# DeltaNet into soft MoE on one core: another order of VectorE's routing work and of the inverse's shares

## The chip, the cores and the metric

The kernel runs on one core of a Trainium2 chip. The metric is the device time of one execution in microseconds. A core has five engines that run side by side, each through its own queue in a fixed order: TensorE (PE, matrix products, with its weight loads as PEld), VectorE (DVE), ScalarE (ACT), GpSimd (POOL), and SyncE (SP), which here issues the DMA loads. An instruction that must wait for another engine holds up all that stands behind it in its own queue.

## The reference, cut to what matters

Two layers follow each other. The first is DeltaNet, a linear attention with a state that is corrected at every token, for 4 batches of 8 heads, 768 tokens and a head size of 48:

```python
k_n = k / (np.linalg.norm(k, axis=-1, keepdims=True) + 1e-06)
for t in range(S):
    y[:, :, t] = np.einsum('bhd,bhde->bhe', q[:, :, t], state)
    v_old = np.einsum('bhde,bhd->bhe', state, kt)
    state = state + bt[..., None] * np.einsum('bhd,bhe->bhde', kt, vt - v_old)
```

Its output, 3072 tokens of 384 numbers, is x of a soft mixture of experts with 8 experts of 4 slots:

```python
logits = x @ phi                                  # 3072 x 32
d = softmax(logits, axis=0)                       # over tokens, for each slot
slot_input = d.T @ x                              # 32 x 384
slot_out[e] = relu(slot_input[e] @ w1[e]) @ w2[e] # 384 -> 1024 -> 384
c = softmax(logits, axis=1)                       # over slots, for each token
out = c @ slot_out
```

(The two softmax lines are written short here; the reference subtracts the maximum, takes exp and divides by the sum plus 1e-9.)

## The kernel before

**Chunks and groups.** The 768 tokens are cut into 24 chunks of 32. The recurrence inside a chunk is written as a triangular system, so that a chunk needs one inverse for each of the 32 pairs of batch and head. Four chunks make a group (six groups, NG = 6), and one group's 4 x 32 inverses, of 32 x 32 each, are made at once on 128 partitions. Between chunks a state S is carried.

**A slot.** The main loop runs over x = 0 to 23. Slot x computes chunk x; c = x mod 4 is its place in the group. `chunk` (its functions stand in the listing) gives the steps of a chunk's own chain:

- `rest`: TensorE multiplies keys by the state (L481, into psR), then R = V - that product is formed. Where `turned_sign` holds, TensorE first adds -V into psR (L494) and ScalarE copies R (L498); elsewhere VectorE subtracts (L500). In groups 1 to 4 VectorE makes R at c = 0 and 1, ScalarE at c = 2 and 3; in group 0 it is the other way round; in group 5 VectorE always makes it.
- `read`: queries by the state (L481, into psY).
- `solve`: the inverse by R (L507, into psR), which ScalarE copies as U (L510).
- `update`: keys by U (L520, into psS), which ScalarE copies as the new state S (L527, two instructions). The next slot's `rest` needs it.
- `outputs`: the chunk's inner product (L537), copied by ScalarE as Y (L540).

Around this chain a slot prepares chunk x + 8 (transposes L261, products of keys and queries L290, their copies by ScalarE), scales the values of chunk x + 2 on GpSimd (`scale_v`, L442), masks the weights of chunk x + 1 on GpSimd (`weights`, L450), and copies the inverse of the next chunk on ScalarE (`solvers`, L458, from TT to Tbs).

**The inverse of a group on VectorE.** `invert(n)` makes some 90 small products and subtractions (lines 368 and 373: functions ea, es, ma, ms, then la, ls) in a fixed order. Before them come `spread` (a transpose of 128 x 1024 into lb, L325), `root` on ScalarE and `norms` (L343 to L355); two transposes into TT (`back`, L433) end it. `clear` sets the tile nm to zero on GpSimd once VectorE has last read it.

The inverse of group n + 2 is prepared at the last slot of group n (`spread`, `clear`, `root`) and its steps run in the four slots of group n + 1. The table `share` says what part of its estimated work stands at each of three places of each of the four slots; `plan` deals the steps out by it. The first place stands at the head of a slot, ahead of `rest`; the second after `solve`; the third later, with the hook "vec" in its middle. `norms` stands at the first slot's second place. What the shares leave over stands at the last slot's second place.

**Routing.** When a group's Y is complete, `route` works on its logits over the next six slots, as a list of six dictionaries: the entry's number is the slot after the group, its key the hook in the slot at which the functions are called. The hooks' order in a slot is head, (`rest`, `read`), sums, (`solve`), act, mid, vec, (`update`, `outputs`), end. On VectorE are `maxima` (L591, L592), `run_max` (L618, L622), `over_slots` (L628, L629), `shares` (L638 to L641) and `collect` (L703 to L707). ScalarE makes `rows_exp` and `slots_exp` (L648, L653, L634) of what run_max and over_slots give; shares sum and divide what slots_exp gives. `over_rows` (L597) and `slots` (L688) are products on TensorE.

The program's order is the order in which these calls are made: a manual schedule, with no planner that moves instructions. The loop calls them so:

```python
drain(EL[c][0]); hook("head")
rest(); read(); hook("sums"); solve()
...
hook("act"); drain(EL[c][1])
...
hook("mid"); drain(EL[c][2][:cut]); hook("vec"); drain(EL[c][2][cut:])
...
update(); outputs(); later(x, 2); hook("end")
```

After the loop come the two layers of the experts (L1038, L1061) and the output (L1119), whose weights are loaded into buffers as the loop sets them free.

Of the kernel before, what the change touches and what calls it, by code (L numbers as in the profile page):

```python
# [17 lines left out]
def kernel(  # L18
# [54 lines left out]
    def pt(shape):  # L73
        return ps.tile(shape, F32, name="pt", tag="pt", bufs=2)
# [490 lines left out]
    def route(n, Yn, yT, cs=range(GC), turn=None, behind=False):  # L565
# [114 lines left out]
        def slots(cs):  # L680

            pa = st["pa"] = [psS[:, cs[0] + y, 0:GD + 1] if n == NG - 1 else pt([P, GD + 1])
                             for y in range(2)]
            for c in cs:
                for b in range(B):
                    for y in range(2):
                        r, o = slice(64 * y, 64 * y + 64), slice(64 * (b % 2), 64 * (b % 2) + 64)
                        nc.tensor.matmul(  # L688
                            pa[y][o], lhsT=st["dr"][r, c * B + b].rearrange("p x s -> p (x s)"),
                            rhs=Yn[r, c, b, 0:GD + 1], start=(c == cs[0] and b < 2),  # L690
                            stop=(c == cs[-1] and b >= 2), skip_group_check=True)

            if not straight:
                st["pac"] = small.tile([P, 2, GD + 1], F32, name="pac", tag="pac", bufs=1)
                for y in range(2):
                    nc.scalar.activation(st["pac"][:, y], pa[y], ACT.Copy)

        def collect(first):
            parts = [(sacc[:, y], st["pa"][y]) for y in range(2)] if straight else [
                (sacc, st["pac"])]  # L700
            for s, pa in parts:
                if not first:
                    nc.vector.tensor_tensor(s, s, pa, op=ALU.add)  # L703
                elif turn == 0:
                    nc.vector.tensor_copy(s, pa)
                else:
                    nc.vector.scalar_tensor_tensor(s, s, st["al"], pa, op0=ALU.mult, op1=ALU.add)  # L707


        if n < NG - 2:  # L710
            return [dict(end=[logits]),
                    dict(head=[maxima], mid=[by_tokens], end=[over_rows]),
                    dict(head=[run_max, over_slots], end=[rows_exp, slots_exp]),
                    dict(act=[shares], end=[repeat, heads]),
                    dict(sums=[lambda: slots((0, 1))], vec=[lambda: collect(True)]),
                    dict(sums=[lambda: slots((2, 3))], vec=[lambda: collect(False)])]
        if n == NG - 2:
            return [dict(end=[logits]),
                    dict(act=[maxima], mid=[over_rows, by_tokens], vec=[run_max, over_slots],
                         end=[rows_exp, slots_exp]),  # L720
                    dict(act=[repeat, heads], vec=[shares],
                         mid=[lambda: slots((0, 1)), lambda: collect(True)],
                         end=[lambda: slots((2, 3)), lambda: collect(False)])]
# [14 lines left out]


    PLACES = 3  # L740
    share = [(0.0, 0.07, 0.16), (0.11, 0.10, 0.11), (0.09, 0.09, 0.09), (0.09, 0.09, 0.0)]

    def plan(n):

# [127 lines left out]
    def ends(x, name):  # L872

        if (x, name) == (NCH - 2, "end"):
            two[0] = route(NG - 1, Ys[1], yT[NG - 1], (0, 1), NG - 1)
            two[0]["logits"]()
        elif x == NCH - 1:
            for f in dict(head=["maxima"], act=["over_rows", "run_max", "rows_exp"],
                          mid=["repeat"], end=["heads"]).get(name, ()):
                two[0][f]()  # L880

    for x in range(NCH):
        n, c = divmod(x, GC)
        if c == 0 and n:
            routing[n - 1] = route(n - 1, Ys[(n - 1) % 2], yT[n - 1])
# [67 lines left out]
        if c == GC - 1:  # L953
            EL = empty
            if follow:
                f, EL = follow
                f["clear"]()
                f["root"]()

    rb = route(NG - 1, Ys[1], yT[NG - 1], (2, 3), NG, behind=True)  # L960
    Cn = [Call[:, i].rearrange("p b s -> p (b s)") for i in range(NG)]
    cT = cpool.tile([P, NG * P], F32, name="cT")
# [215 lines left out]
```

## Time and profile before

| what | value |
|---|---|
| time, median of 3 | 337.31 us (336.77 to 347.18) |
| the profiled execution | 342.02 us, span 340.3 us |
| TensorE busy | 280.8 us (83%) |
| VectorE busy | 212.2 us (62%) |
| ScalarE busy | 172.1 us (51%) |
| GpSimd busy | 155.9 us (46%) |
| mean granted TensorE clock | 0.876 |

A row of the timeline gives the start in us, the time that the instruction (or the merged run of equal ones, with its count) took, engine, line, operation, tiles and shapes; in brackets is how long the engine had sat idle before it, and what ended that. A row of the list of waits gives the waiting engine, line and tile, the engine and line waited for, and then the total in us, how often, and the longest in us. "PEclk" is the share of full clock that TensorE was granted, by fortieths of the span on the page (in tenths) and by stretch in the table of windows. PEld is the load of a matmul's stationary operand, which overlaps the matmuls; a wait can stand under PE and under PEld at once.

### The profile page before, as it was taken

What the parts mean: (1) busy time and instruction counts of PE and PEld (TensorE: products, weight loads), DVE (VectorE), ACT (ScalarE), POOL (GpSimd) and SP (SyncE); (2) the same over time, 40 slices, a digit from 0 to 9 for tenths busy, and PEclk for the clock granted to TensorE, in tenths of its full rate; (3) what the DMA queues carried; (4) which work ended last, traced back from release to release, by engine and by line L of the source; (5) the groups of instructions that cost most, each with busy time, mean ns of one, the idle gap of its engine ahead of it and who ended that gap; (6) DMA issues with size and microseconds to landing.
All of it is one profiled execution on the core that took longest, in us unless ns stands there. A gap on an engine that the chain in (4) does not pass through costs nothing.

```text
span 340.3 us, 16627 instructions
## 1 busy us (share of the span) xinstructions
PE 280.8 (83%) x7081; PEld 226.3 (66%) x7081; DVE 212.2 (62%) x807; ACT 172.1 (51%) x386; POOL 155.9 (46%) x336
## 2 busy tenths in 40 slices
PE   3996688888969889599886998939997888999981
PEld 3774476776858778477775877828876766636651
DVE  8599939875994478936769475697751221314341
ACT  3354254667724778156782646915475673221141
POOL 8966376559276078750599113994672000000000
PEclk9998559999965999759998589995799998999996
DMA  7866555454443246514520255526499559975196
GB/s 142 153 99 94 82 86 90 76 82 69 70 78 58 48 67 127 122 32 114 86 65 19 44 143 156 158 87 173 108 320 327 157 181 320 329 216 187 32 307 221
DMA packets 96378, 45.28 MB, mean 133 GB/s; under 512 B 75440, under 2 KB 89808, under 8 KB 96304
## 3 DMA queue, kind: packets, MB, share of 16 engines
q1 hardware_dynamic: 94512, 42.98, 50.9%
q0 software_dynamic: 704, 1.03, 1.6%
q8 instruction: 56, 0.92, 1.1%
q10 hardware_dynamic: 1088, 0.20, 0.3%
q14 instruction: 18, 0.15, 0.2%
HBM read 39.47 MB, written 4.72 MB: 130 GB/s over the span
## 4 chain that ended last, share of the span: by engine, by line
PE 53%; ACT 19%; DVE 16%; issue 4%; DMA 4%; POOL 1%; SPq 0%; DVEq 0%; POOLq 0%; ACTq 0%
PE psR L507 9%; PE psS L520 6%; PE pt L290 5%; DVE prs L368 5%; ACT S L527 5%; PE pt L261 4%; PE psY L537 4%; PE pt L558 4%; PE pso L1061 3%; PE ph L1038 3%; DVE prs L373 3%; PE psR L481 3%; ACT Tbs L458 2%; ACT dr L678 2%; PE psR L494 2%
## 5 line engine op out<-in xcount | busy, mean ns | idle before, releaser
L442 POOL TENSOR_SCALAR Vs<-Vs,nT 128x48 f32<-128x48 f32 x192 | 86.6, 475 | 24.0 <-DMA Vs<-in_v_dram 14.0
L450 POOL TENSOR_SCALAR_AFFINE_SELECT Abs<-GQ 32x256 f32<-32x256 f32 x96 | 48.2, 502 | 29.1 <-PE psY L537 24.4
L373 DVE TENSOR_TENSOR prs<-prs 128x16 f32<-128x16 f32 (+15 forms) x186 | 55.2, 297 | 0.4
L507 PE MATMUL psR<-R,Tbs 64*64 64x48 f32 x768 | 32.0, 241 | 20.5 <-DVE R L500 14.8
L368 DVE TENSOR_TENSOR prs<-tt,lb 128x96 f32<-128x96 f32 (+21 forms) x186 | 47.0, 290 | 0.0
L507 PEld LDWEIGHTS psR<-R,Tbs 64*64 64x64 f32 x768 | 28.9, 155 | 24.8 <-DVE R L500 16.4
L527 ACT ACTIVATE S<-psS 48x768 f32<-48x768 f32 x46 | 36.9, 803 | 8.7 <-PE psS L520 8.3
L510 ACT ACTIVATE U<-psR 128x384 f32<-128x384 f32 x24 | 11.8, 491 | 48.7 <-PE psR L507 42.4
L290 PE MATMUL pt<-KQ 48*32 48x64 f32 (+1 forms) x1792 | 27.2, 243 | 4.7 <-ACT KQ L277 3.2
L537 PE MATMUL psY<-U,Abs 64*64 64x48 f32 x768 | 30.5, 234 | 0.0
L537 PEld LDWEIGHTS psY<-U,Abs 64*64 64x64 f32 x768 | 27.4, 149 | 2.6 <-issue 0.8
L290 PEld LDWEIGHTS pt<-KQ 48*32 48x32 f32 x1792 | 21.8, 122 | 9.7 <-ACT KQ L277 5.0
L368 DVE TENSOR_TENSOR prs<-tt,prs 128x240 f32<-128x240 f32 (+14 forms) x90 | 26.0, 294 | 0.0
L320 POOL MEMSET prs<- 128x256 f32 x6 | 1.9, 314 | 51.4 <-DVE prs L368 51.4
L481 PEld LDWEIGHTS psR<-S,KQ 128*32 128x32 f32 x768 | 18.1, 120 | 10.8 <-ACT S L527 4.1
L373 DVE TENSOR_TENSOR tt<-tt,prs 128x30 f32<-128x30 f32 (+7 forms) x90 | 24.6, 273 | 0.0
L458 ACT ACTIVATE Tbs<-TT,own 128x256 f32<-128x256 f32 x48 | 21.6, 501 | 5.8 <-DVE TT L433 5.8
L481 PE MATMUL psY<-S,KQ 128*32 128x96 f32 x768 | 22.5, 256 | 2.0 <-issue 2.0
L481 PE MATMUL psR<-S,KQ 128*32 128x96 f32 x768 | 23.1, 267 | 1.0 <-ACT S L527 0.8
L294 ACT ACTIVATE GQ<-pt 128x256 f32<-128x256 f32 (+1 forms) x56 | 16.8, 351 | 13.2 <-PE pt L290 13.1
L558 PE MATMUL pt<-ident,Y 128*96 128x128 f32 x96 | 17.3, 306 | 6.8 <-ACT GQ L294 5.9
L261 PE MATMUL pt<-ident,Q 128*128 128x128 f32 x72 | 20.3, 315 | 0.0
(230 smaller groups left out, 602.5 us busy)
## 6 DMA issues: line engine op xcount, KB each, us to landing
Q<-in_q_dram SPq DMA_DIRECT2D x96, 48.0 KB, 2.8
wKQ<-in_moe_w_dram SPq DMA_DIRECT2D x16, 256.0 KB, 3.5
Vs<-in_v_dram SPq DMA_DIRECT2D x80, 48.0 KB, 2.6
wGQ<-in_moe_w_dram SPq DMA_DIRECT2D x12, 256.0 KB, 4.0
Ka<-in_k_dram SPq DMA_DIRECT2D x40, 48.0 KB, 2.8
w<-in_moe_w_dram SPq DMA_DIRECT2D x6, 256.0 KB, 3.1
Ka<-in_moe_w_dram SPq DMA_DIRECT2D x8, 192.0 KB, 3.5
S<-in_moe_w_dram SPq DMA_DIRECT2D x8, 192.0 KB, 4.5
```

What stands on the lines that cost most here:

```text
L261: nc.tensor.transpose(dst, self.src[a][:, b * G:(b + 1) * G, :].rearrange("p g d -> p (g d)"), ident)
L290: nc.tensor.matmul(pg[g][rh, b], lhsT=kq[r, b, 0, rh], rhs=kq[r, b, a0:a1, rh], start=True, stop=True, skip_group_check=True)
L368: nc.vector.tensor_tensor(pr, a.broadcast_to([P] + shape), b.broadcast_to([P] + shape), op=ALU.mult)
L373: nc.vector.tensor_tensor(dst, dst, pr, op=op)
L442: nc.gpsimd.tensor_scalar(Vt[cc][:, u], Vt[cc][:, u], nT[n][:, c * U + u:c * U + u + 1], None, op0=ALU.mult)
L450: nc.gpsimd.affine_select(out=Ab[cc % NT][r, :, h % 2, :].rearrange("p (b g) t -> p b g t", g=G), in_=GQ[n][r, c, :, :, 1, :], compare_op= ...
L458: nc.scalar.activation(Tb[cc % 2][:, :, x, :], TT[n][:, c * U:(c + 1) * U, :], ACT.Identity, scale=own[:, x:x + 1])
L481: nc.tensor.matmul(dst[hs[h], b].rearrange("p g d -> p (g d)"), lhsT=kq[:, b, a, hs[h]], rhs=old[:, h, b, :], start=((a == 1 or not turned ...
L507: nc.tensor.matmul(pw[half[y], u], lhsT=T[y][:, u], rhs=st["R"][half[y], u], start=(u == 0), stop=True, skip_group_check=True)
L527: nc.scalar.activation(new[r, :, :, g * D:(g + 1) * D], psS[r, :, 0:B * GD].rearrange("p h (b g e) -> p h b g e", b=B, g=G)[:, :, :, g], A ...
L537: nc.tensor.matmul(qs[half[y], b, g], lhsT=at[y][:, u], rhs=st["U"][half[y], u], start=False, stop=True, skip_group_check=True)
L558: nc.tensor.transpose(py[:, b, :], Yn[:, c, i + b, 0:GD], ident)
```

## The change

VectorE's work of routing moves behind more of the inverse, and the inverse's work is dealt out otherwise over the four slots. In the first four routings `maxima` moves from ahead of R to behind it in the second slot, `run_max` and `over_slots` move from the head of the third slot to its "vec" hook, and `shares` moves from the fourth slot to the end of the "vec" hook of the fifth. The slots' parts of the inverse go from 23, 32, 27 and 18 to 16, 29, 33 and 22 per cent; the second slot's first place, ahead of R, becomes empty. It is meant to leave less work ahead of R on VectorE where R is due, and to place work that waits for other engines behind work that does not.

```diff
         if n < NG - 2:
             return [dict(end=[logits]),
-                    dict(head=[maxima], mid=[by_tokens], end=[over_rows]),
-                    dict(head=[run_max, over_slots], end=[rows_exp, slots_exp]),
-                    dict(act=[shares], end=[repeat, heads]),
-                    dict(sums=[lambda: slots((0, 1))], vec=[lambda: collect(True)]),
+                    dict(act=[maxima], mid=[by_tokens], end=[over_rows]),
+                    dict(vec=[run_max, over_slots], end=[rows_exp, slots_exp]),
+                    dict(end=[repeat, heads]),
+                    dict(sums=[lambda: slots((0, 1))], vec=[lambda: collect(True), shares]),
                     dict(sums=[lambda: slots((2, 3))], vec=[lambda: collect(False)])]
...
-    share = [(0.0, 0.07, 0.16), (0.11, 0.10, 0.11), (0.09, 0.09, 0.09), (0.09, 0.09, 0.0)]
+    share = [(0.0, 0.05, 0.11), (0.0, 0.14, 0.15), (0.13, 0.10, 0.10), (0.12, 0.10, 0.0)]
```

## The prediction

> **What bounds the kernel now.** I read the page's engine rows first: no engine is full (TensorE 83%, VectorE 62%), so the order of work sets the time. Second, the list of waits, for TensorE waiting on another engine inside the loop. Third, TensorE's timeline, to see at which slot that wait falls. Fourth, busy time per slot. I call a slot x = 0 to 23, c = x mod 4 its place in the group of four, and let it begin with its solve (L507).
>
> The page's slices give the clock, the list of waits the reason:
>
> ```profile
> PEclk9998559999965999759998589995799998999996
> ```
>
> and, with the waiting engine first,
>
> ```profile
> PEld psR L507 <- DVE R L500: 16.4, 7, 5.5
> PE psR L507 <- DVE R L500: 14.8, 5, 5.3
> ```
>
> The solve waits for R from VectorE, and the granted clock dips at five places of the loop. The two rows tell much the same waits, once for matmuls and once for weight loads. TensorE's timeline at slots 9, 13 and 17, all c = 1:
>
> ```profile
> 140.93 1.94 PE L507 MATMUL psR<-R,Tbs 64*64 64x48 f32 x32 [3.35 <-DVE R L500]
> ...
> 185.37 1.94 PE L507 MATMUL psR<-R,Tbs 64*64 64x48 f32 x32 [3.16 <-DVE R L500]
> ...
> 229.57 1.94 PE L507 MATMUL psR<-R,Tbs 64*64 64x48 f32 x32 [5.34 <-DVE R L500]
> ```
>
> The same 32 matmuls take 1.14 us in slot 7. Slot 5 has the wait too (2.75 us). Busy time by slot, columns span, PE, PEld, DVE, ACT, POOL, granted clock, DMA share, GB/s; rows are slots 7 to 10:
>
> ```profile
> 119.05:128.25 9.20, 8.31 (x273) 7.31 (x273) 6.18 (x19) 6.82 (x14) 6.88 (x18) 1.00 0.43 70
> 128.25:140.93 12.68, 8.81 (x307) 7.77 (x301) 11.99 (x52) 6.72 (x18) 10.37 (x21) 0.97 0.57 113
> 140.93:154.83 13.90, 13.44 (x241) 11.11 (x241) 8.51 (x37) 6.43 (x14) 6.88 (x12) 0.54 0.36 76
> 154.83:163.60 8.77, 7.93 (x242) 6.44 (x238) 4.48 (x18) 6.81 (x15) 0.00 (x0) 1.00 0.49 113
> ```
>
> Slot 8 ends with VectorE full (11.99 of 12.68) and TensorE waiting; slot 9 then runs whole at 0.54 of the clock. So each c = 1 slot costs twice: the stall, and a slot at half clock. VectorE's timeline says what keeps R:
>
> ```profile
> 135.39 0.27 DVE L368 TENSOR_TENSOR prs<-tt,lb 128x96 f32<-128x96 f32 x1
> 135.59 0.27 DVE L373 TENSOR_TENSOR tt<-tt,prs 128x120 f32<-128x120 f32 x1
> ...
> 139.81 0.27 DVE L591 TENSOR_REDUCE m<-lT 128x1 f32<-128x128 f32 x1
> 140.12 0.26 DVE L592 TENSOR_SCALAR m<-hm,m 128x4 f32<-128x4 f32 x1
> 140.32 0.56 DVE L500 TENSOR_TENSOR R<-Vs,psR 128x384 f32<-128x384 f32 x1
> ...
> 152.10 0.22 DVE L618 TENSOR_SCALAR_CACHE_REDUCE neg<-pmc,nrun 128x4 f32<-128x4 f32 x1 [5.28 <-ACT pmc L601]
> ...
> 163.20 0.28 DVE L638 TENSOR_REDUCE sm<-el 128x4 f32<-128x128 f32 x1 [4.26 <-ACT el L634]
> ```
>
> R stands behind inverse and maxima with no gap, though TensorE's state product (L481 into psR, 135.22 + 0.87) was there at 136.1. Later VectorE idles 5.28 and 4.26 us, because run_max and shares stand ahead of inverse that could have run.
>
> **What the Trainium skill says.** "TensorE: Matmul & The Clock Gate", What's actually happening: after an idle window of about 3.4 us TensorE falls to half clock, and about as much sustained work frees it; the window runs freely. The trace agrees on half clock (0.54 in slots 5, 9 and 13, 0.50 in 17), but stalls of 2.75 and 3.16 us tip it as well, and it stays low for a whole slot. "Perfetto Trace Analysis", Optimizing Scalar/DVE Operations: VectorE and GpSimd share an SBUF read port, so their work can slow each other. The trace fits: eight V scalings (L442) take 3.03 us at 121.41 and 4.07 us at 132.75, beside a full VectorE.
>
> **The change part by part.** No instruction is added or removed; VectorE's order changes.
>
> (1) Less inverse ahead of R at c = 1. Work ahead falls from 0.07 + 0.16 + 0.11 = 0.34 to 0.05 + 0.11 = 0.16, and maxima go behind R. In the built order 16 inverse instructions and two of maxima leave; the trace has them at 135.59 to 140.32: 4.73 us (slot 13: 180.05 to 184.76, slot 17: 224.20 to 228.96). R now names ScalarE among its waits; maxima's own wait had covered it. Of ScalarE's work before R nothing ends after 135.92 at slot 9, so I take 0.
>
> (2) shares (four instructions, 163.20 to 164.15 = 0.95 us) go ahead of R at slots 9, 13 and 17, not at 5 (the first routing starts at 4).
>
> What R can win is the least of what VectorE frees and what TensorE still has to do:
> - Slot 5: psR is ready at 92.96, VectorE at 91.67. R 0.56 plus a hand-over of 0.05 gives a solve at 93.65, against 96.37: 2.7 us.
> - Slot 9: R at 140.32 - 4.73 + 0.95 = 136.5, done 137.1; L688 holds TensorE to 137.58. Against 140.93: 3.35 us.
> - Slot 13, the same way: L688 ends at 182.2, against 185.37: 3.15 us.
> - Slot 17: R at 225.15, solve at 225.75, against 229.57: 3.8 us. TensorE is free at 224.23, so a gap of 1.5 us stays; smaller than any that tipped the clock.
> Sum 13.0 us.
>
> (3) With gaps of 0 to 1.5 us I expect full clock. The c = 1 slot then does the work of the next slot plus L607 and L597 (0.33 + 0.28 by their full-clock rows, some 0.5 overlapped): 8.65 + 0.5 = 9.15 against 14.03, 13.90 and 13.87, so 4.9 + 4.75 + 4.7. Slot 17: 7.15 + 0.5 = 7.65 against 11.46, 3.8, and 0.65 for the slow first solve of slot 18 (1.79, not 1.14). Sum 18.8 us.
>
> (4) run_max and over_slots behind more inverse in c = 2. Queued behind is ScalarE: rows_exp, slots_exp, then R of c = 3 (L498), then the solve. After R at slot 9 VectorE has maxima 0.5, the moved 4.2, the old rest of the slot 6.0 (140.79 to 146.8) and 2.1 of the next: it meets run_max at 149.9 and is through at 150.9. ScalarE came to rows_exp at 162.16, now 3.35 + 4.75 = 8.1 sooner: 154. No cost; hidden behind U, S and Y on ScalarE. In slot 14 the same sum gives 195.3 against 198.4. In slot 18, where no later chunk is prepared, it gives 225.7 + 0.5 + 4.25 + 6.0 + 2.4 + 0.9 = 239.75 against 225.75 + 7.65 + 5.05 (246.74 less 241.03, less 0.65) = 238.45: **+1.3 us**.
>
> (5) 0.33 and 0.22 of the inverse in slots c = 2 and 3. VectorE's work of a group, from norms at 128.70 to R at 171.04 without the idle 5.28, 4.26 and 1.62, is 31.2 us: it ends at 159.9. TensorE reaches the next c = 0 R at 170.9 - 8.1 = 162.8. Slack 2.9 us; TT is done at 157.6, and ScalarE wants it (L458) at 163.6. Cost 0. GpSimd's clear of nm waits for VectorE's last la, which keeps its place to the next solve. Cost 0.
>
> (6) Group 0 (slots 0 to 3): R is on ScalarE at c = 0 and 1; at 2 and 3 slightly less stands ahead of it (0.58 for 0.64, 0.90 for 0.91) and VectorE was idle there (1.21 and 1.86 us). Cost 0.
>
> Sum: 13.0 + 18.8 - 1.3 = 30.5 us.
>
> **From which time it goes off.** The profiled execution took 342.02 us and has all four half-clock slots; the recorded times 336.77, 342.02 and 347.18 lie 5.2 apart, one such slot each. So I take the median, 337.31, to hold three of the four: it wins 30.5 - 4.7 = 25.8, or 311.5, the same as 342.02 - 30.5. If it held all four: 306.8. I give 311.
>
> **The rivals.**
> - B, stalls go, half clock stays (some other gap tips it): 337.3 - 13.0 + 1.3 = 325.6. For it: stalls under 3 us tipped the clock before. Against it: TensorE has at most 1.5 us left at these places, and slots 6 and 7, with gaps of about half a microsecond, are at 1.00.
> - C, VectorE becomes the bound. A group takes about 36 us instead of 44.4, and the 31.2 us of VectorE work meet the same GpSimd work in less time. Instructions already vary (128x120 subtraction 0.28 or 0.34). If sharing stretches it by 15%, 4.7 us, slack 2.9 is gone and each of three groups loses 1.8, and slot 17 with its short slots about 2: 311 + 7 = 318.
> - D, slower. R would really wait for something the trace puts down wrongly (for one R of slot 5 it names a DMA), the stalls stay, shares add 0.95 at three slots, and each c = 3 solve waits 1.3 for ScalarE: 337.3 + 2.9 + 5.2 = 345. Against it: VectorE has no gap before R in slots 9, 13 and 17.
>
> **How the numbers follow.** Likeliest 0.72 at 311 (304 to 316); C 0.11 at 318; B 0.11 at 326; D 0.06 at 345. The low end is all four half-clock slots won (307) less a little in slots 18 to 20; the high end takes in C and some of B: 303 to 323. B and D left out are 0.17. Faster by over 2% means under 330.6: 0.93; D leaves 0.05 slower, and 0.02 stay between.
>
> **What would show it.** Right: no wait of L507 on R over 2 us at c = 1; clock near 1.00 in slots 5, 9, 13 and 17, and spans near 9 us (slot 17 near 7.7); VectorE without its 5 us and 4 us gaps before L618 and L638. Step 4: a wait of ScalarE on VectorE at slot 18. Wrong: the clock still near 0.54 there (B), R at c = 0 waiting for VectorE's transpose (C), or L507 waiting for R of ScalarE at c = 3 in every group (D).

## The result, and the profile after

The changed kernel takes 313.57 us (median of 4 runs, 311.43 to 316.95), the kernel before 337.31 (336.77 to 347.18): a ratio of 0.928, 95% interval 0.920 to 0.936. The prediction was 311. The profiled executions took 312.60 and 342.02 us, 29.4 apart; the readings below are of these two. The ratio leaves out executions over 1.5% above the fastest of their kernel, and the profiled one of the kernel before is such a slow one, 4.7 us over its median, with no trace of a faster one at hand.

The page of the changed kernel, granted clock by slices, and further down the chain of work that ended last, by engine:

```profile
PEclk9999566999999999999999999999799998999985
...
PE 47%; DVE 24%; ACT 16%; issue 3%; DMA 3%; SPq 2%; POOL 2%; DVEq 0%; POOLq 0%; ACTq 0%
```

Of the five dips of the loop one is left whole (slot 0 and what stands just ahead of it, the slices 5, 6, 6) and a short one is new (the 7, in slot 19). TensorE has gone from 53% of the chain to 47, and VectorE from 16 to 24.

From the list of waits of the changed kernel, in the order engine, tile and line waiting, what it waited for, total us, times, longest us:

```profile
PE psR L507 <- ACT R L498: 8.3, 4, 4.2
...
ACT dT L648 <- DVE neg L618: 3.5, 2, 2.6
...
PE psR L507 <- DVE R L500: 2.9, 3, 2.3
...
DVE neg L618 <- ACT pmc L601: 2.2, 1, 2.2
```

The solve's wait for VectorE's R has fallen from 14.8 us to 2.9, of which 2.33 lie at slot 17. Its wait for ScalarE's R, 5.2 us before, is 8.3 now: 4.19 of them at slot 0, and 3.03, which are new, at slot 19. VectorE's own idle time is gone as well: 18.9 us ahead of run_max (L618) have become 2.2, and 17.2 ahead of shares (L638) 0.8. A new row has come: ScalarE's rows_exp (L648) waits for run_max, 2.6 us of it at once.

Busy time by slot of the changed kernel, columns as before, for slots 8, 9 and 16 to 19:

```profile
120.14:129.26 9.12, 8.60 (x307) 7.76 (x302) 8.33 (x41) 6.33 (x16) 6.07 (x15) 1.00 0.56 123
129.26:138.97 9.71, 8.42 (x253) 6.82 (x242) 9.68 (x41) 6.72 (x16) 7.76 (x11) 1.00 0.57 120
...
192.68:202.54 9.86, 7.39 (x236) 6.25 (x229) 9.10 (x38) 5.10 (x14) 9.31 (x22) 1.00 0.54 150
202.54:208.88 6.34, 6.34 (x170) 5.25 (x170) 6.30 (x27) 4.58 (x10) 6.16 (x12) 1.00 0.65 168
208.88:218.13 9.25, 6.14 (x170) 4.89 (x167) 9.11 (x32) 5.27 (x11) 8.88 (x18) 1.00 0.89 260
218.13:226.53 8.40, 8.16 (x200) 7.00 (x200) 6.52 (x26) 5.13 (x9) 3.17 (x8) 0.80 0.75 244
```

Slot 8 took 12.68 us with TensorE idle for 3.9 of them, and takes 9.12; slot 9 ran at 0.54 of the clock for 13.90 us, and runs at 1.00 for 9.71. In slots 16 to 18 the VectorE column nearly fills the span (24.5 of 25.45 us). VectorE at the end of slot 8 shows why R comes sooner:

```profile
127.65 0.47 DVE L368 TENSOR_TENSOR prs<-tt,lb 128x120 f32<-128x120 f32 x2
128.08 0.56 DVE L500 TENSOR_TENSOR R<-Vs,psR 128x384 f32<-128x384 f32 x1
128.55 0.28 DVE L591 TENSOR_REDUCE m<-lT 128x1 f32<-128x128 f32 x1
```

R follows the inverse's product of 128x120, as soon as the state product that it needs is there (127.96), and maxima (L591) follow R. R is done at 128.64; TensorE is at L688 until the solve at 129.26 and waits for nothing.

By slots, all from such windows of the two profiled executions (a slot runs from its solve to the next):

| slots | before, us | after, us | won |
|---|---|---|---|
| 4, 8, 12, 16 (these end with the wait for R) | 11.23, 12.68, 12.65, 13.14 | 8.54, 9.12, 9.75, 9.86 | 12.4 |
| 5, 9, 13, 17 (at half clock before) | 14.00, 13.90, 13.87, 11.46 | 8.94, 9.71, 8.93, 6.34 | 19.3 |
| 18, 19, 20 | 7.15, 7.02, 9.27 | 9.25, 8.40, 7.82 | -2.0 |
| all others of 0 to 22 | 111.98 | 111.82 | 0.2 |

The sum is 29.9; ahead of the first solve and behind slot 22 the two spans differ by 0.4 the other way.

### The profile page after: what moved, and what is told of

It reads as the page before. It is cut to its first block, busy times and chain, and to the rows that moved or that the text cites. A ratio compares the mean times of both kernels' runs of the same rounds, so it can differ in the third digit from the quotient of the medians.

```text
span 310.8 us, 16635 instructions
## 1 busy us (share of the span) xinstructions
PE 261.1 (84%) x7081; PEld 209.0 (67%) x7081; DVE 216.3 (70%) x807; ACT 171.7 (55%) x386; POOL 159.2 (51%) x336
## 4 chain that ended last, share of the span: by engine, by line
PE 47%; DVE 24%; ACT 16%; issue 3%; DMA 3%; SPq 2%; POOL 2%; DVEq 0%; POOLq 0%; ACTq 0%
DVE prs L368 9%; PE psR L507 6%; DVE prs L373 5%; PE psS L520 5%; PE pt L290 5%; ACT S L527 4%; PE pso L1061 3%; PE ph L1038 3%; PE pt L558 3%; PE pt L261 3%; DVE tt L373 3%; PE psY L537 2%; ACT dr L678 2%; PE psR L481 2%; PE po L1119 2%
## 5 line engine op out<-in xcount | busy, mean ns | idle before, releaser
L442 POOL TENSOR_SCALAR Vs<-Vs,nT 128x48 f32<-128x48 f32 x192 | 89.7, 491 | 22.9 <-DMA Vs<-in_v_dram 6.9
L507 PE MATMUL psR<-R,Tbs 64*64 64x48 f32 x768 | 28.6, 226 | 11.8 <-ACT R L498 8.3
L507 PEld LDWEIGHTS psR<-R,Tbs 64*64 64x64 f32 x768 | 25.7, 140 | 15.6 <-ACT R L498 10.0
L290 PE MATMUL pt<-KQ 48*32 48x64 f32 (+1 forms) x1792 | 26.0, 234 | 5.4 <-ACT KQ L277 3.2
L537 PE MATMUL psY<-U,Abs 64*64 64x48 f32 x768 | 27.4, 220 | 0.2 <-issue 0.2
L537 PEld LDWEIGHTS psY<-U,Abs 64*64 64x64 f32 x768 | 24.3, 134 | 2.8 <-issue 0.7
L373 DVE TENSOR_TENSOR tt<-tt,prs 128x30 f32<-128x30 f32 (+7 forms) x90 | 26.0, 288 | 0.0
L481 PEld LDWEIGHTS psR<-S,KQ 128*32 128x32 f32 x768 | 16.4, 112 | 8.8 <-ACT S L527 4.6
L481 PE MATMUL psR<-S,KQ 128*32 128x96 f32 x768 | 21.2, 253 | 1.0 <-ACT S L527 0.8
L500 DVE TENSOR_TENSOR R<-Vs,psR 128x384 f32<-128x384 f32 x14 | 7.7, 553 | 18.7 <-PE psR L481 7.1
```

What stands on the lines that cost most here:

```text
L290: nc.tensor.matmul(pg[g][rh, b], lhsT=kq[r, b, 0, rh], rhs=kq[r, b, a0:a1, rh], start=True, stop=True, skip_group_check=True)
L373: nc.vector.tensor_tensor(dst, dst, pr, op=op)
L442: nc.gpsimd.tensor_scalar(Vt[cc][:, u], Vt[cc][:, u], nT[n][:, c * U + u:c * U + u + 1], None, op0=ALU.mult)
L481: nc.tensor.matmul(dst[hs[h], b].rearrange("p g d -> p (g d)"), lhsT=kq[:, b, a, hs[h]], rhs=old[:, h, b, :], start=((a == 1 or not turned ...
L507: nc.tensor.matmul(pw[half[y], u], lhsT=T[y][:, u], rhs=st["R"][half[y], u], start=(u == 0), stop=True, skip_group_check=True)
L537: nc.tensor.matmul(qs[half[y], b, g], lhsT=at[y][:, u], rhs=st["U"][half[y], u], start=False, stop=True, skip_group_check=True)
```

## The experiments

Times are medians, ratios those of the runs beside the kernel before on the same chip (median 339.9 us beside the first four kernels, 341.0 beside the others). The theory T was the prediction's: R at c = 1 came late because inverse stood ahead of it, and the idle gap put the next slot at half clock. It leaves three things open: which part of the change does it, whether the half clock is indeed the price of the gap, and what bounds slots 16 to 19 now.

**The table alone.** The changed kernel with the routing places of the kernel before:

```diff
-                    dict(act=[maxima], mid=[by_tokens], end=[over_rows]),
-                    dict(vec=[run_max, over_slots], end=[rows_exp, slots_exp]),
-                    dict(end=[repeat, heads]),
-                    dict(sums=[lambda: slots((0, 1))], vec=[lambda: collect(True), shares]),
+                    dict(head=[maxima], mid=[by_tokens], end=[over_rows]),
+                    dict(head=[run_max, over_slots], end=[rows_exp, slots_exp]),
+                    dict(act=[shares], end=[repeat, heads]),
+                    dict(sums=[lambda: slots((0, 1))], vec=[lambda: collect(True)]),
```

> The new table of shares alone; the routing functions stand where they stood before. Theory (the order ahead of R at c = 1 is what counts, and the table alone empties it): maxima (0.5 us) stay ahead of R, shares do not come ahead of it, so R of slot 9 comes some 4.2 us sooner than before and the solve is held only by TensorE's own L688. All four half-clock slots go. run_max at the head of slot 18 costs no wait of ScalarE, so slots 18 and 19 take about 7 us each, not 9.25 and 8.40: 308 to 312 us, at or below the changed kernel. Rival (the moved routing work brings a good part): VectorE idles ahead of run_max and shares as before, the inverse ends later, R at c = 0 or the copies of TT wait, 320 to 328 us.

Measured: 315.55 us (314.44 to 317.49), ratio 0.940 (0.928 to 0.952). Its busy time by slot, slots 9, 19 and 20:

```profile
132.66:141.80 9.14, 8.39 (x252) 6.83 (x242) 9.11 (x41) 6.72 (x16) 5.96 (x11) 1.00 0.58 122
...
216.86:228.81 11.95, 7.10 (x200) 5.85 (x200) 11.14 (x37) 5.30 (x11) 7.95 (x17) 0.94 0.74 239
228.81:237.94 9.13, 9.12 (x229) 8.29 (x230) 1.40 (x4) 4.49 (x10) 1.81 (x4) 0.70 0.78 257
```

Slots 5, 9, 13 and 17 run at full clock with the table alone (8.93, 9.14, 8.90 and 6.35 us). Over slots 1 to 22 this kernel takes 194.3 us, the changed one 194.0. So the table brings all that single executions can tell apart (the changed kernel's second profile, further down, has 192.9). The time lies above the 308 to 312 that I gave it; its profile shows two reasons: slot 0 took 17.11 us in this execution (14.53 in that of the changed kernel, with the same order there), and the lateness of slots 16 to 19 shows in another place: slot 20's solve waits 4.15 us for the copy of an inverse that VectorE transposed only at 226.78, and slot 20 then runs at 0.70.

**The routing alone.** The new places of routing with the old table:

```diff
-    share = [(0.0, 0.05, 0.11), (0.0, 0.14, 0.15), (0.13, 0.10, 0.10), (0.12, 0.10, 0.0)]
+    share = [(0.0, 0.07, 0.16), (0.11, 0.10, 0.11), (0.09, 0.09, 0.09), (0.09, 0.09, 0.0)]
```

> The routing functions in their new places with the old table. Theory: 0.34 of the inverse still stands ahead of R at c = 1, and shares (0.95 us) come on top at slots 9, 13 and 17 while maxima (0.5 us) leave: stalls of 3 to 6 us and half clock in slots 5, 9, 13 and 17 remain, 335 to 341 us. Rival (the moved routing work brings a good part): 320 to 328 us.

Measured: 333.74 us (331.29 to 341.15), ratio 0.990 (0.976 to 1.003). TensorE's timeline at the solves of slots 5, 9 and 17 (slot 13 waits 3.02 us):

```profile
98.81 1.13 PE L507 MATMUL psR<-R,Tbs 64*64 64x48 f32 x32 [2.00 <-DVE R L500]
...
137.62 1.14 PE L507 MATMUL psR<-R,Tbs 64*64 64x48 f32 x32 [2.69 <-DVE R L500]
...
224.29 1.95 PE L507 MATMUL psR<-R,Tbs 64*64 64x48 f32 x32 [5.20 <-DVE R L500]
```

All four waits are still there, 0.1 to 0.75 us shorter than before. That little decided one slot: after 2.00 us slot 5 stayed at full clock (8.94 us, before 14.00 after a gap of 2.75), while slots 9 and 13 ran at 0.60 and 0.53. The routing alone does not remove the wait; what it gains depends on which gaps tip the clock in an execution, and its interval includes 1. VectorE's idle time ahead of run_max and shares goes with either half of the change (3.9 and 0.8 us are left here, 2.2 and 1.5 with the table alone, of 18.9 and 17.2), so it is not what the time hung on.

**The half clock without the wait removed.** The kernel before with matmuls of an identity, one every 0.12 us, ahead of four solves; they add nothing to the output and fill TensorE's gap, while R comes as late as it did. T says that this wins the half-clock slots (19 us) and leaves the stalls (12 to 13):

```diff
+    def feed(k):
+        for _ in range(k):
+            nc.tensor.matmul(psS[:, 0, 384:512], lhsT=ident, rhs=ident, start=False, stop=True,
+                             skip_group_check=True)
...
         hook("sums")
+        feed({5: 11, 9: 14, 13: 13, 17: 22}.get(x, 0))
         solve()
```

> The kernel before, with 11, 14, 13 and 22 extra matmuls of the identity (into columns of psS that nothing reads) between the routing product and the solve at slots 5, 9, 13 and 17, so that TensorE works through most of its wait for R. R comes no sooner. Theory (the half clock is the price of the idle gap): the stalls stay, the four slots run at full clock, 317 to 324 us. Rival (the half clock has another cause, such as the mix of work in that slot): 335 to 340 us, clock near 0.54 there.

Measured: 322.64 us (320.5 to 327.2), ratio 0.957 (0.942 to 0.972). Its busy time by slot, slots 8, 9 and 17:

```profile
127.32:139.87 12.55, 12.03 (x336) 10.95 (x329) 11.86 (x54) 6.73 (x18) 10.15 (x21) 1.00 0.56 112
139.87:148.81 8.94, 8.24 (x243) 6.80 (x242) 6.56 (x30) 6.34 (x14) 7.31 (x13) 1.00 0.36 87
...
218.47:224.83 6.36, 6.36 (x170) 5.25 (x170) 6.33 (x25) 4.59 (x10) 4.29 (x8) 1.00 0.66 176
```

Slots 4, 8, 12 and 16 are as long as in the kernel before (50.5 us together, before 49.7), but the four that follow take 33.2 instead of 53.2. So the half clock was the price of TensorE's idle gap: with the gap filled and R as late as before, it is gone. It was the larger part: 20 us, against 12 for the stalls themselves. The whole time fell by less than 20 (by 14.8 from one profiled execution to the other), since in this one slot 0 took 3.0 us more than before and slot 21 ran at 0.53 (10.20 us, before 6.99).

**Step 4 at slot 18.** The new row of waits asks whether run_max at the "vec" hook costs slots 18 and 19. The timeline of the changed kernel, VectorE, ScalarE and TensorE in order of time:

```profile
213.54 0.49 ACT L540 ACTIVATE Y<-psY 128x384 f32<-128x384 f32 x1
...
216.43 0.20 DVE L618 TENSOR_SCALAR_CACHE_REDUCE neg<-pmc,nrun 128x4 f32<-128x4 f32 x1
...
216.68 0.72 ACT L648 ACTIVATE dT<-lT,nrun 128x512 f32<-128x512 f32 x1 [2.64 <-DVE neg L618]
...
217.61 0.47 ACT L498 ACTIVATE R<-psR 128x384 f32<-128x384 f32 x1
...
218.13 1.60 PE L507 MATMUL psR<-R,Tbs 64*64 64x48 f32 x32 [3.03 <-ACT R L498]
```

run_max comes behind a run of inverse; ScalarE, done with Y at 214.03, idles 2.64 us for it and has R queued behind; TensorE idles 3.03 us for that R, and its 32 matmuls then take 1.60 us, the mark of the lower clock. The experiment puts run_max back to the head, in this one routing alone:

```diff
-                    dict(vec=[run_max, over_slots], end=[rows_exp, slots_exp]),
+                    dict([("head" if n == NG - 3 else "vec", [run_max, over_slots])],
+                         end=[rows_exp, slots_exp]),
```

> The changed kernel, with run_max and over_slots of the fourth routing alone put back to the head of slot 18. Theory: ScalarE's 2.6 us wait on run_max goes (VectorE would reach it about 213.3 us, and be done by 214.2, when ScalarE comes to it at 214.0), and with it the 3.0 us stall of the solve of slot 19 and its half clock: 3 to 4 us less, 309 to 311 us. Rival (VectorE is the bound there anyway, and R of slot 20 or the copies of TT wait instead): 313 us, no change.

Measured: 317.53 us (316.71 to 318.37), ratio 0.944 (0.935 to 0.953). Busy time of slots 17 and 18:

```profile
206.26:216.94 10.68, 10.68 (x169) 8.62 (x169) 10.57 (x47) 4.80 (x10) 8.81 (x16) 0.55 0.56 153
216.94:223.67 6.73, 6.38 (x171) 5.13 (x167) 6.66 (x18) 5.15 (x11) 5.20 (x10) 0.96 0.55 155
```

ScalarE's wait is gone, and slots 18 to 20 take 23.0 us instead of 25.5: step 4's mechanism is right. The kernel is no better for it. In the profiled execution that is slot 17's doing: the gap ahead of its solve was 2.85 us (2.33 in the changed kernel's), and slot 17 ran at 0.55, 10.68 us for 6.34. Of the other three runs, all above 316 us as well, only the times are known. One gap that may or may not tip the clock hides an effect of 2 us.

**The changed kernel again,** as a control beside the next three:

> The changed kernel once more, as the measure for the three that run beside it on the same chip. Slots 1 to 17 as in its first trace. The first slot of the loop took 14.5 us in the two first traces and 17.1 to 17.4 us (clock 0.50) in the four experiments, and a gap of 2.3 to 2.9 us ahead of slot 17 tipped the clock in one of two kernels with the same order up to there. Both theories expect 312 to 318 us, by which of these fall to half clock.

Measured: 313.61 us (312.95 to 313.72), ratio 0.931 (0.921 to 0.941). With not one instruction different, slot 17's gap was 2.72 us this time and the slot 7.86 us at 0.78; slots 18 and 19 took 6.84 and 7.84; slot 0 took 17.11. Gaps of 2 to 3 us, and what they cost, differ between executions of one kernel.

**A smaller share ahead of slot 17.** Rival: not the order but VectorE's work as a whole bounds slots 16 to 19, so that what is taken from one place shows at the next. The kernel with run_max at the head of slot 18, and with 11, 29, 35 and 25 per cent for the last inverse alone:

```diff
+    last = [(0.0, 0.04, 0.07), (0.0, 0.14, 0.15), (0.13, 0.10, 0.12), (0.14, 0.11, 0.0)]
...
-                total += share[c][p] * whole
+                total += (last if n == NG - 1 else share)[c][p] * whole
```

> The changed kernel with run_max and over_slots of the fourth routing at the head of slot 18, and a table of its own for the last inverse (slots 16 to 19): 11, 29, 35 and 25 per cent, so that some 1.1 us less stand ahead of R at slot 17. Theory (VectorE is only late at slots 17 and 18, it has room in slot 19): the gap ahead of slot 17 falls under 2 us and stays at full clock, slot 16 takes about 8.9, slot 17 6.4, slot 18 6.6, slot 19 7.0 to 7.5 us: 4 to 6 us less than the changed kernel on the same chip. Rival (VectorE's work of slots 16 to 19 is a bound as a whole): what is won at slots 17 and 18 comes back as a wait for TT ahead of slot 20, as in the run of the table alone: no more than 1 us less.

Measured: 316.38 us (313.26 to 317.91), ratio 0.936 (0.918 to 0.955). Its timeline where slot 19 ends:

```profile
226.42 1.04 DVE L433 STREAM_TRANSPOSE TT<-tt 128x512 f32<-128x512 f32 x1
...
227.49 0.91 ACT L458 ACTIVATE Tbs<-TT,own 128x256 f32<-128x256 f32 x2 [4.82 <-DVE TT L433]
...
228.45 1.84 PE L507 MATMUL psR<-R,Tbs 64*64 64x48 f32 x30 [4.60 <-ACT Tbs L458]
```

The gap at slot 17 shrank to 0.36 us and slot 16 to 8.44, as meant. Then the inverse came late: ScalarE waits for its transpose, the solve of slot 20 for ScalarE, 4.60 us, and slot 20 runs at 0.58. Slots 16 to 20 take 44.1 us, in the changed kernel 41.7 and in its second profile 40.6. The rival's forecast came true: what was won at slots 16 to 18 came back at slots 19 and 20.

**Feeding what gaps are left.** The changed kernel with 9, 9 and 11 such matmuls ahead of the solves of slots 0, 17 and 19; and the kernel just before with 9 and 5 ahead of slots 0 and 17:

```diff
+        feed({0: 9, 17: 9, 19: 11}.get(x, 0))
         solve()
```

> The changed kernel with 9, 9 and 11 extra matmuls of the identity ahead of the solves of slots 0, 17 and 19, where TensorE still idles 4.2, 2.3 and 3.0 us; no other work is moved. Theory (half clock is the price of the gap and of nothing else): the gaps' lengths stay, slot 0 runs mostly at full clock (14.5 or 17.3 to some 12 us), slot 17 never at half clock, slot 19 at 7.0 instead of 8.4: 3 to 7 us less than the changed kernel on the same chip. Rival: the clock of slot 0 depends on other work and stays near 0.5 to 0.7; 1 to 2 us less.

> Both together: the two edits of VectorE's order at slots 16 to 19, and 9 and 5 extra matmuls ahead of the solves of slots 0 and 17. Theory: the gains add, since they lie in different slots: 7 to 10 us less than the changed kernel on the same chip, 304 to 308 us. Rival: as much as the better of the two alone.

Measured: 313.19 us (311.4 to 314.51), ratio 0.930 (0.917 to 0.942), and 314.86 us (312.37 to 315.68), ratio 0.934 (0.921 to 0.947): neither differs from the control's 0.931, so the 3 to 7 and 7 to 10 us that were to be won did not come. In the first, slots 0, 19 and 21:

```profile
42.87:58.89 16.02, 14.30 (x306) 11.46 (x306) 12.15 (x60) 7.49 (x17) 10.27 (x16) 0.59 0.51 90
...
220.58:227.61 7.03, 6.72 (x201) 5.73 (x200) 6.29 (x26) 5.13 (x9) 3.59 (x8) 1.00 0.78 269
...
234.48:244.20 9.72, 7.28 (x178) 6.50 (x168) 1.78 (x7) 5.50 (x14) 0.00 (x0) 0.82 0.58 186
```

Slots 17 and 19 are at full clock, as meant, and slots 16 to 20 take 39.6 us, 1.0 to 2.1 less than without. But slot 21 loses 2.7 us (it took 6.99 in all other profiles but one, the 10.20 above), part of it at a lower clock, and nothing is left. Slot 0 stayed at 0.59, though only 1.16 us of its gap remained. In the second kernel slot 0's gap was still 5.91 us, and slot 20 waited for the late inverse again (2.94 us, then 0.70).

None of these kernels is shown to be faster than the changed one.

## Why the prediction was right

**Steps 1 and 2, less inverse ahead of R.** Predicted 2.7, 3.35, 3.15 and 3.8 us for the stalls ahead of slots 5, 9, 13 and 17 (13.0); measured, as the shortening of slots 4, 8, 12 and 16, 2.7, 3.6, 2.9 and 3.3 (12.4). The cap that was used, what TensorE itself still has to do, was the right one: at slot 9 L688 does end last. (For slot 5 the sum as written comes to 93.57, not 93.65; the queries' product held TensorE to 93.62, so nothing changes.) At slot 17, where no such cap exists, a gap of 1.5 us was to stay, and 2.33 did: VectorE came to R 9.26 us behind slot 16's solve, where 8.72 had been reckoned, and TensorE was free 0.27 us sooner than reckoned. So the sign "no wait of L507 on R over 2 us at c = 1" did not come true there, and slot 17's full clock was luck: with the same order up to it, gaps of 2.72 and 2.85 us in two later executions put it at 0.78 and 0.55. The table alone has these gains and the routing alone does not.

**Step 3, the clock.** Predicted 18.2 us in slots 5, 9, 13 and 17; measured 19.3, all four at 1.00, so rival B is out. That the half clock came of the gap is shown by the fed kernel, where R is as late as before and the clock full. Slot 17 was put too long: 7.65 us were built from slot 18's 7.15, although 0.65 of these were the slow first solve that the same step takes off slot 18, and it took 6.34.

**Step 4, ScalarE behind run_max at slot 18.** This is the term that was mis-sized. Predicted was a cost of 1.3, less 0.65 for a faster first solve in slot 18: 0.65. Slots 18 to 20 cost 2.0. The wait took place where it was put (none such in groups 1 to 3), but at 2.64 us for ScalarE and 3.03 for TensorE. Counted from slot 17's solve, rows_exp could start at 14.1 us, where 14.0 had been reckoned; but ScalarE was there at 11.5 and not at 12.7, since slot 17 was 1.3 us shorter than step 3 had it. What step 3 won there beyond its forecast came back as this wait. And a gap of 3.03 us had its own price: slot 19 ran at 0.80. I had counted a wait once where step 3 counts it twice. In the second profile, where slot 17 took 7.86 us, ScalarE came to rows_exp at 218.55 and started it at 218.67, with no wait to speak of, and slots 18 to 20 took 22.85 us, less than the 23.44 of the kernel before; the size of this term is thus not settled to better than 2 us.

**Steps 5 and 6, and rival C.** Groups 1 to 3 cost little through VectorE: the R of c = 0 does not wait for the transposes, and the longest wait of a solve for R is 0.43 us, at slot 13. In slots 16 to 19, though, VectorE is busy 31.0 of 33.9 us, and there C fits: the experiments at slots 17 and 18 moved the lateness from R to run_max to the transposed inverse and back, and won nothing.

**The base.** Taking 342.02 as the execution with all four half-clock slots gave 311.5; the profiled execution of the changed kernel took 312.60. The terms sum to 29.9 where 30.5 was said, and 0.4 was lost outside the slots. That the median, 337.31, holds three of the four was a guess, and no trace shows it: among the runs of the kernel before beside the experiments, one took 334.18 us and one 342.1 at mean clocks of 0.874 and 0.878, so its time does not simply count spells at half clock. From median to median the change won 23.7 us where 25.8 was said; that 311 came so near is in part luck.

**Rival D** fell with the first view: of the waits for R at slots 5, 9 and 13, which it had stay, 0.43 us at slot 13 is left.

**Open.** Slot 0 takes 14.4 to 14.5 us at 0.71 in some executions and 17.1 to 17.4 at 0.50 or 0.51 in others, of the changed kernel too; these are 2.7 us of the spread between runs. In the former the half clock ends at 51.3 or 51.4 us, in the latter at 59.9 to 61.1; why there, wasn't found. What TensorE waits for in slot 21 of the fed changed kernel (1.88 us that the trace lists as "issue") and at the end of slot 20 of the fed kernel before (1.71 us, in the middle of L688) was not followed up. The two halves of the table's effect, ahead of c = 1 and in slots c = 2 and 3, weren't tried apart.

## What to carry to other kernels

Work without a deadline goes behind what another engine waits for, and an instruction that waits for others goes behind work that could run meanwhile. Where TensorE idles for about half of a 3.4 us step of its clock (the next section has the figures), price the gap twice, as the gap and as the spell at half clock behind it; and read the next slot's clock beside the wait. Before moving work about inside a late stretch, add up the busy time of each engine over the whole of it: where one is full, moving work only chooses which wait shows.

## What the hardware showed that I had not expected

The gap that tips the clock can be shorter than the 3.4 us that the Trainium skill gives ("TensorE: Matmul & The Clock Gate", What's actually happening). All waits of over 0.35 us ahead of solves in slots 5, 9, 13, 17, and those with a late R or inverse at 19 and 20, in all the profiles, with the mean clock of the slot that follows:

| gap, us | clock of the slot that it opens |
|---|---|
| 0.36, 0.37, 0.43, 0.59, 0.62, 0.71, 1.01, 1.69, 2.00, 2.33 | 1.00 each |
| 2.69, 2.72, 2.75, 2.85 | 0.60, 0.78, 0.53, 0.55 |
| 2.94, 3.02, 3.03, 3.16, 3.35 | 0.70, 0.53, 0.80, 0.54, 0.54 |
| 4.15, 4.60, 5.20, 5.34 | 0.70, 0.58, 0.76, 0.50 |

In this table nothing up to 2.33 us tipped it and everything from 2.69 on did. But the length of the gap is not the rule: the two pauses of 1.71 and 1.88 us inside slots, named under "Open", were followed by half clock as well (slot 21 at 0.53 and 0.82). What does sort the cases is the record of the clock itself. It has only the values 1.00 and 0.50, and in all ten profiles it changes only at the edges of equal steps of 3.413 us that run on through the whole execution. The kernel before around its 2.75 us gap ahead of slot 5, step by step (columns as in the other tables):

```profile
92.33:95.74 3.41, 1.29 (x64) 1.07 (x52) 3.05 (x15) 0.49 (x2) 0.00 (x0) 1.00 0.57 87
95.74:99.15 3.41, 2.78 (x96) 2.69 (x96) 3.38 (x14) 0.49 (x1) 3.38 (x8) 0.50 0.33 55
99.15:102.57 3.42, 2.96 (x42) 2.24 (x24) 3.42 (x11) 2.21 (x6) 3.18 (x6) 0.50 0.50 83
102.57:105.98 3.41, 3.41 (x64) 3.15 (x59) 0.43 (x2) 2.23 (x5) 3.31 (x9) 0.50 0.20 35
105.98:109.39 3.41, 3.41 (x32) 2.33 (x35) 1.81 (x8) 1.01 (x3) 1.82 (x5) 0.50 0.41 71
109.39:112.81 3.42, 2.96 (x145) 2.57 (x138) 3.42 (x12) 1.48 (x4) 0.00 (x0) 1.00 0.47 76
```

After a step with TensorE busy 1.29 of 3.41 us the clock is halved, and it stays so for four steps. From the first solve to slot 23's, over the ten profiles, each of the 15 steps at full clock with TensorE busy for 0.51 of the time or less was followed by half clock, none with 0.67 or more was, and of 12 between these two were. So it matters where a gap falls: an edge at 201.51 us cut the changed kernel's 2.33 us gap at slot 17 and left steps busy for 0.58 and 0.70, while the 1.71 us pause fell within one step and left 0.50. An estimate from the 0.51: a gap of 1.7 us can tip the clock when it falls within one step.

How long the spell lasts does not follow the gap either. Half clock never ended behind a step with TensorE busy for 0.90 or less (45 such steps); of 44 steps that were full (0.99 or more), 25 ended it. After 5.20 us the second step at half clock was full and ended the spell, which left slot 17 at 0.76; after 2.75 us, as shown, two steps at 0.81 and 0.87 came first and then two full ones, and slot 5 took 14.00 us. Why one full step ends the spell at times and at times two or more are needed, these traces do not show. TensorE's busy time in a trace is in part modelled, so the shares are approximate. Slot 0, whose clock in the fed changed kernel fell behind a step of 0.63 that began within the 1.16 us gap, is left out of the table of gaps.

In one comparison VectorE also worked faster where GpSimd worked less beside it. From norms to R at slot 9 it took 11.62 us in the kernel before, with GpSimd busy 9.89 of them, and 10.95 in the kernel with the routing alone, with GpSimd busy 6.59, though the instructions that moved add some 0.45 us to that stretch (shares 0.95, less maxima 0.5). That fits the shared port that the prediction names; no run isolates it.
